# 44 small products behind TensorE's last one, ahead of its closing branch

## The chip, the cores and the metric

The kernel runs on one core of one Trainium2 chip. The metric is the device time of one execution in microseconds. The kernel before was run three times; the times given are the median of these runs and their lowest and highest.

## The reference

Attention with normalised queries and keys over 8 batches, 12 heads, 448 tokens and 64 numbers a head, and behind it a two-layer network on the 768 columns of all heads together. Cut to what matters:

```python
def rmsnorm(x, g):
    return x / np.sqrt(np.mean(x * x, axis=-1, keepdims=True) + 1e-06) * g
scores = (1 / np.sqrt(64)) * rmsnorm(q, g_q) @ rmsnorm(k, g_k).transpose(0, 1, 3, 2)
attn = softmax(scores)                       # over the keys
x = (attn @ v)                               # [8, 12, 448, 64] -> [8, 448, 768]
xn = (x - mean(x)) / np.sqrt(var(x) + 1e-06) * g_ln
out = x + np.maximum(xn @ w_ch1, 0) @ w_ch2  # 768 -> 3072 -> 768
```

## The kernel before

The order of all engines' instructions is written out by hand. A first part (`run_first`) does the attention of the first batch from a written list; it also holds small products of the identity with itself (line 532, tile `psW`). A second part (`run_rest`) goes through the eight batches: for each, it emits the chunks of the network (`mlp_chunks`) and, between them, the steps of the next batch's attention (`upto`). TensorE computes scores (L405), attention times values (L458, L460), the first layer (L798, tile `psH`) and the second (L821, tile `psP`). ScalarE does the exponentials (L421) and the ReLU (L801), VectorE the additions (L757, L804), and stores go out from SP's queue, ScalarE's and GpSimd's (L956, L959).

The last batch has no attention beside it. In `run_rest` its chunks are emitted one after the other (the branch `if b + 1 == B`), and then the loop ends. Its last group of tokens (`mlp_group` with `final`) closes with one product cut in two halves of 192 columns: 12 products each (L821), each half followed by one addition on VectorE (L757) and by a store in two parts, one from SP and one from ScalarE (L959).

In two of these chunks, `flag` computes whether all intermediate values stayed within the limits for which this fast way holds. It writes one whole number (`sh.flag`); its last step is a product into a tile `psF` with the tag `oB` of the PSUM pool `ps_o` (L1035) and a comparison on VectorE (L1036).

Behind `run_rest`, each of the five engines loads the flag into a register (L1218, `nc.values_load`) and takes a branch (L1219, `tc.If`). With the flag at 0, as here, the branch skips the general path `_general`, whose code stands in the program between the fast way and the closing code. Behind the branch, each engine has an instruction that waits until its own earlier instructions are done. SP then waits, one after the other, for all DMAs and all engines' counts, and all five meet at a barrier (both under L1246). The program ends behind a second such barrier. A hint for the branch (`mark_branch_hint_location`) is called among the last chunks; in the built program, and in the trace, the five hints stand at the start of the streams (L1246, at 0.9 to 1.0 us).

In the profile's rows, PE is TensorE's product unit, PEld its weight loads and PEldq or PEq its instruction stream; DVEq, ACTq, POOLq and SPq are the streams of the other engines.

Of the kernel before, what the change touches and what calls it, by code (L numbers as in the profile page):

```python
# [8 lines left out]
FP32 = mybir.dt.float32  # L9
# [17 lines left out]
EXP_BIAS = -4.0  # L27
DVE_KG, POOL_HI, POOL_DUP, ACT_Q = (0, 6), (1, 2, 3, 4, 5, 6, *range(8, 25)), (3, 4, 5, 6), (0, 2, 4, 5)
POOL_SQUARE, POOL_LO = ((2, 1), (4, 0), (6, 0)), (5, 6)

# [59 lines left out]
class _Fast:  # L92
# [870 lines left out]
    def upto(self, target):  # L963
        while self.pos < min(target, len(self.steps)):
            for call in self.steps[self.pos]:
                call()
            self.pos += 1
# [8 lines left out]
    def run_rest(self):  # L976
        steps, mark, upto = self.steps, self.mark, self.upto
        for b in range(B):
            tail = TAIL[b]
            chunks = list(self.mlp_chunks(b))  # L980
            total = sum(c for c, _ in chunks)
            if b + 1 == B:
                for i, (_, emit) in enumerate(chunks):
                    if i == len(chunks) - 55:
                        self.tc.mark_branch_hint_location("general", "LikelyTaken", [ENG.PE, ENG.DVE, ENG.SP, ENG.Activation, ENG.Pool])
                    for call in emit if isinstance(emit, list) else [emit]:
                        call()
                    if i in FLAG_AT:
                        self.flag(FLAG_AT.index(i))
                break  # L990
            start, goal = self.pos, mark[b + 1]
            done, items = 0.0, None
            if b == 0:
                ops, last = self.weight_sums()
            elif b == 1:
                ops += last
            left = sum(c > 0 for c, _ in chunks)
            for cost, emit in chunks:
                if not cost:
                    emit()  # L1000
                    continue
                for i, call in enumerate(emit):
                    call()
                    if i + 1 < len(emit):
                        upto(int(min(goal, start + (goal - start) * (done + cost / 2) / (total - 960 * tail))))
                left -= 1
                if (left < 10 if b == 0 else b == 1) and ops:
                    ops.pop(0)()
                done += cost
                upto(int(min(goal, start + (goal - start) * done / (total - 960 * tail))))  # L1010
                if self.pos >= goal:
                    if items is None:
                        items = self.ln_list(b + 1)
                        if b == 0:
                            items.insert(items.index("X1") + 1, "y8")
                            self.ln["y8"] = self.prep_ops(8)["y"]
                        for u, (x, _, _) in enumerate(UNITS):
                            if x == b + 2 and self.late_v(u):
                                self.ln[f"Z{u}"] = self.prep_ops(u)["z"]
                                items.append(f"Z{u}")  # L1020
                    if items and (items[0][0] != "X" or left <= DOWN):
                        x = items.pop(0)
                        self.ln[x]()
            for x in items:
                self.ln[x]()
            if b + 2 == B:
                upto(len(steps))
# [223 lines left out]
```

## Time and profile before

| | us |
|---|---|
| median of 3 runs | 581.99 |
| lowest and highest | 581.73, 582.49 |
| profiled execution, its own time | 579.58 |
| span of the profiled execution, first to last instruction | 578.0 |
| TensorE busy | 559.5 (97%) |
| VectorE busy | 381.7 (66%) |
| ScalarE busy | 364.4 (63%) |
| GpSimd busy | 207.0 (36%) |

Busy times count computing instructions; loads of registers, branches, waits and the issue of DMAs are not in them. All times in rows are microseconds from the first instruction, unless a row says otherwise. The profiled execution's own time is 1.6 us longer than its span, and the runs without a profile are 2.4 us longer than that.

The rows of the fetch of instructions (queues `q8` and `q14`, kind "instruction") give packets, megabytes and the share of 16 DMA engines' time. Where such a row is shown for a stretch of time, the share is of that stretch.

### The profile page before, as it was taken

Reading aid. Unit: us, or ns where it says so; the run is one execution under the profiler, and the core shown is the slowest. Engines: PE = TensorE matmul, PEld = TensorE weight load, DVE = VectorE, ACT = ScalarE, POOL = GpSimd, SP = SyncE. Lnnn points to the kernel's source line nnn. Section 1 sums busy time; section 2 is a strip of 40 time slices with the busy share of each in tenths; the row PEclk is TensorE's granted clock in tenths of the full one; section 3 lists DMA queues with packets and bytes.
Section 4 is the critical chain, followed back from the end, with each engine's and each line's share of the span. In section 5 each row is a group of like instructions: output and inputs, shape, how many; then the busy total and the mean of one; then the engine's idle time right before and its main releaser. Section 6 shows DMA issues by size and latency. Waiting matters only on the chain.

```text
span 578.0 us, 13670 instructions
## 1 busy us (share of the span) xinstructions
PE 559.5 (97%) x5446; PEld 411.9 (71%) x5446; DVE 381.7 (66%) x826; ACT 364.4 (63%) x674; POOL 207.0 (36%) x224
## 2 busy tenths in 40 slices
PE   5788999999999999999999999999999999999997
PEld 4556666687686867777677768777777777878684
DVE  6989567699657586845667586854756743664424
ACT  5998787447675779557775588637777477323130
POOL 5885636404440620654241521644242320020000
PEclk9999999999999999999999999999999999999999
DMA  8999999958672876969663798958743390030201
GB/s 206 251 238 222 214 207 165 193 147 137 124 131 77 158 127 145 127 148 121 121 106 48 184 134 136 128 143 122 145 64 65 119 113 1 1 110 1 83 2 58
DMA packets 178329, 72.59 MB, mean 126 GB/s; under 512 B 138212, under 2 KB 173220, under 8 KB 178260
## 3 DMA queue, kind: packets, MB, share of 16 engines
q1 hardware_dynamic: 133876, 52.52, 44.1%
q0 software_dynamic: 43440, 18.52, 25.2%
q8 instruction: 44, 0.72, 0.5%
q10 hardware_dynamic: 944, 0.62, 0.4%
q14 instruction: 25, 0.20, 0.1%
HBM read 52.76 MB, written 11.01 MB: 110 GB/s over the span
## 4 chain that ended last, share of the span: by engine, by line
PE 77%; DVE 1%; issue 0%; DVEq 0%
PE psH L798 33%; PE psP L821 30%; PE psS L405 7%; PE oA L458 4%; PE oB L460 1%; PE psS L411 1%; DVE qn L83 0%; DVE w2s L763 0%; DVE ssq L265 0%; DVE w L763 0%; DVE xn L662 0%; DVE hS L804 0%; DVE x L475 0%; DVE xl L757 0%; DVE xl L480 0%
## 5 line engine op out<-in xcount | busy, mean ns | idle before, releaser
L421 ACT ACTIVATE E<-psS,rr_all 128x448 f16<-128x448 f32 x336 | 204.6, 634 | 47.3 <-PE psS L405 40.3
L798 PE MATMUL psH<-xnT,w 128*128 128x256 f16 (+1 forms) x2016 | 225.7, 261 | 0.0
L798 PEld LDWEIGHTS <-w 128*128 128x128 f16 x2016 | 172.8, 98 | 24.3 <-issue 4.9
L801 ACT ACTIVATE hS<-psH 128x512 f16<-128x512 f32 x150 | 89.8, 599 | 97.2 <-PE psH L798 93.0
L821 PEld LDWEIGHTS <-hS 128*128 128x128 f16 x1080 | 100.0, 98 | 57.3 <-issue 1.1
L821 PE MATMUL psP<-w,hS 128*128 128x384 f16 x672 | 127.0, 326 | 0.0
L405 PE MATMUL psS<-qU,kU 128*128 128x448 f16 x288 | 100.9, 352 | 5.0 <-ACT E L421 3.2
L458 PEld LDWEIGHTS <-E 128*128 128x128 f16 x1008 | 70.3, 98 | 35.8 <-issue 2.8
L279 POOL TENSOR_TENSOR k<-k,gprod 128x896 f32<-128x896 f32 x18 | 38.9, 2160 | 139.5 <-ACT khl L259 113.2
L804 DVE TENSOR_TENSOR hS<-hS 128x512 f16<-128x512 f16 (+1 forms) x119 | 60.2, 512 | 19.3 <-ACT hS L801 17.8
L821 PE MATMUL psP<-w2s,hS 128*128 128x384 f16 (+1 forms) x408 | 69.9, 321 | 0.0
L458 PE MATMUL oA<-v,E 128*128 128x65 f16 x864 | 66.9, 193 | 1.1 <-ACT E L421 0.6
L757 DVE SCALAR_TENSOR_TENSOR x<-psP,rs_all,x 128x384 f32<-128x384 f32 x60 | 36.4, 617 | 42.4 <-PE psP L821 41.8
L460 PE MATMUL oB<-v,E 128*128 128x65 f16 x288 | 52.0, 193 | 0.1
L832 POOL TENSOR_TENSOR x<-x,hS 128x384 f32<-128x384 f32 x21 | 23.4, 1126 | 76.1 <-ACT hS L900 75.5
L473 DVE RECIPROCAL rec_all<-oA 128x6 f32<-128x6 f32 x48 | 9.2, 193 | 53.6 <-PE oA L458 53.5
L216 POOL DMA_DIRECT2D v<-in_v_dram x54 | 41.5, 781 | 4.0 <-PE oB L460 2.7
L405 PEld LDWEIGHTS <-kU 128*128 128x128 f16 x288 | 28.0, 98 | 11.1 <-issue 2.2
L900 ACT ACTIVATE hS<-hS,rs_all 128x384 f32<-128x384 f32 x27 | 14.6, 604 | 33.0 <-DVE hS L804 33.0
L460 PEld LDWEIGHTS <-E 128*128 128x128 f16 x336 | 32.4, 96 | 0.4 <-DVE xl L480 0.3
L83 DVE SCALAR_TENSOR_TENSOR qn<-q,rr_all 128x256 f16<-128x256 f32 (+2 forms) x69 | 24.8, 420 | 7.2 <-ACT rr_all L269 7.1
L265 DVE TENSOR_REDUCE ssq<-khl 128x14 f32<-128x896 f32 (+1 forms) x24 | 25.5, 1061 | 5.0 <-ACT khl L259 4.8
(145 smaller groups left out, 616.6 us busy)
## 6 DMA issues: line engine op xcount, KB each, us to landing
k<-in_k_dram SPq DMA_DIRECT2D x19, 384.0 KB, 4.2
q<-in_q_dram SPq DMA_DIRECT2D x18, 384.0 KB, 3.9
out_dram<-x SPq DMA_DIRECT2D x14, 384.0 KB, 3.0
w<-in_moe_w_ch_dram POOLq DMA_DIRECT2D x3, 1536.0 KB, 14.3
v<-in_v_dram POOLq DMA_DIRECT2D x54, 64.0 KB, 4.4
out_dram<-x POOLq DMA_DIRECT2D x9, 384.0 KB, 2.7
w<-in_moe_w_ch_dram POOLq DMA_DIRECT2D x1, 2304.0 KB, 22.5
w<-in_moe_w_ch_dram POOLq DMA_DIRECT2D x2, 1152.0 KB, 14.4
```

What stands on the lines that cost most here:

```text
L216: nc.gpsimd.dma_start(out[:, :, j, 0:D], main[:, :, j])
L265: nc.vector.tensor_reduce(out=c["ssq"][:, n], in_=c["sq", n], axis=AX.X, op=ALU.add)
L279: (nc.vector if u in DVE_KG else nc.gpsimd).tensor_tensor(out=c["t"][1], in0=c["t"][1], in1=sh.gprod.unsqueeze(1).broadcast_to([128, g, D] ...
L405: nc.tensor.matmul(ps[0][:, 0:S], c["main"][:, ts(i, 128)], c["q"][:, ts(h, S)], start=True, stop=True)
L421: nc.scalar.activation(out=o, in_=x[:, 0:S], func=AFT.Exp, scale=self.units[u][3][:, g:g + 1], bias=EXP_BIAS)
L458: nc.tensor.matmul(oA[:, t, cs], E[:, ts(t, 128)], rhs, start=(i == 0 and t == 0), stop=(i == 6 and t == 2))
L460: nc.tensor.matmul(oB[:, cs], E[:, 320:448], rhs, start=(i == 0), stop=(i == 6))
L757: self.nc.vector.scalar_tensor_tensor(out=x, in0=ps, scalar=self.rs[:, b, t:t + 1], in1=x, op0=ALU.mult, op1=ALU.add)
L798: nc.tensor.matmul(ps[:, i], sh.w1[:, dc, ts(f + i, 128)], self.xnT[:, dc, 256 - N:256], start=(i == 0 and dc == 0), stop=(i == k - 1 and ...
L801: nc.scalar.activation(out=hT[:, f:f + k], in_=ps, func=AFT.Relu)
L804: nc.vector.tensor_tensor(out=out, in0=a, in1=c, op=op)
L821: nc.tensor.matmul(bank[x][:, c], a[:, f], w[:, f, c], start=(start and f == 0), stop=(stop and f == HALF - 1))
```

## The change

Behind the last chunk of the last batch, TensorE gets 44 products of the 128x128 identity with itself, each with its weight load: 88 instructions. They write a new tile `psW` of the pool `ps_o` with the tag `oB`, which nobody reads. In the built program they stand behind TensorE's last product and ahead of its load of the flag; TensorE's count of products that it and SP wait for at the end is 44 higher. The streams of the other engines up to their branches are the same.

```diff
+END_WORK = 44
 ...
                     if i in FLAG_AT:
                         self.flag(FLAG_AT.index(i))
+                psW = self.ps_o.tile([128, 128], FP32, tag="oB", name="psW")
+                for _ in range(END_WORK):
+                    self.nc.tensor.matmul(psW, self.sh.id16, self.sh.id16, start=True, stop=True)
                 break
```

In the changed kernel the added products are line 993, and the lines behind the loop stand four further down.

## The prediction

> **What bounds the kernel now.** I read the chain that ended last first, then the end of the timeline, then the closing instructions by line, then the DMA queues in narrow stretches. The page and the chain, in order of time:
>
> ```profile
> span 578.0 us, 13670 instructions
> ...
> PE 77%; DVE 1%; issue 0%; DVEq 0%
> ...
> 564.38 9.79 PE psP L821 x72
> ```
>
> TensorE's products carry the chain to 574.17 us (564.38 + 9.79). What follows is 3.9 us in which no product runs, and the change lies in there. The timeline of the last microseconds (start, length, engine, line, operation):
>
> ```profile
> 572.02 2.14 PE L821 MATMUL psP<-w2s,hS 128*128 128x192 f16 x24
> ...
> 573.65 1.47 SPq L959 DMA_DIRECT2D out_dram<-xl  x2
> 574.20 0.42 DVE L757 SCALAR_TENSOR_TENSOR xl<-psP,rs_all,xl 128x192 f32<-128x192 f32 x1 [0.57 <-PE psP L821]
> ```
>
> The last product ends at 574.16; VectorE's last addition takes 574.20 to 574.62; the last store is issued behind it. Then every engine takes the branch that skips the general path (L1219) and meets at the barrier (L1246). These two lines, as the views of one source line show them (duration in ns min/median/max, first and last start in us):
>
> ```profile
> L1218 PEldq TENSOR_LOAD <-flag x1: 487/487/487, 572.5 to 572.5; - x1
> ...
> L1219 POOLq COMPARE_BRANCH  x1: 67/67/67, 537.1 to 537.1; - x1
> ...
> L1219 PEldq COMPARE_BRANCH  x1: 2287/2287/2287, 573.1 to 573.1; - x1
> L1219 DVEq COMPARE_BRANCH  x1: 84/84/84, 575.1 to 575.1; - x1
> L1219 SPq COMPARE_BRANCH  x1: 78/78/78, 575.2 to 575.2; - x1
> L1219 PEldq EVENT_SEMAPHORE  x1: 51/51/51, 575.5 to 575.5; - x1
> L1219 DVEq EVENT_SEMAPHORE  x1: 21/21/21, 575.7 to 575.7; - x1
> L1219 ACTq COMPARE_BRANCH  x1: 73/73/73, 576.2 to 576.2; - x1
> L1219 ACTq EVENT_SEMAPHORE  x1: 17/17/17, 576.7 to 576.7; - x1
> ```
>
> ```profile
> L1246 PEldq DRAIN  x1: 248/248/248, 575.6 to 575.6; - x1
> ...
> L1246 SPq DRAIN  x2: 7/10/13, 577.1 to 577.2; - x2
> ...
> L1246 POOLq EVENT_SEMAPHORE  x1: 17/17/17, 577.2 to 577.2; - x1
> ```
>
> TensorE's branch takes 2.29 us, where the other engines' take 0.07 to 0.08. Yet TensorE stands at the barrier at 575.9 (575.6 + 0.25). The barrier is passed at 577.2, when SP comes, 1.3 us after TensorE. SP's own waits in the stretch from 574.6 to the end, and the landing of the last two pairs of stores:
>
> ```profile
> SPq L1246 <- DMA out_dram<-xl: 0.3, 1, 0.3
> ...
> DMA to landing us min/median/max: 2.1/2.5/2.9
> ```
>
> So the end is set by VectorE's last addition, the issue of the last store at 574.6 and its landing 2.1 to 2.5 us later. A TensorE that comes to the barrier before 577.2 costs nothing, and one that comes earlier than now gains nothing.
>
> **The change, part by part.** It adds 44 weight loads and 44 products at the end of TensorE's stream, ahead of its load of the flag and its branch. The other engines' streams up to their branches are as they were. The two waits that count TensorE's products (TensorE's instruction behind the branch, and one in SP's list at the barrier) now count 44 more, so both stand behind the last of the added ones. Their output tile was last used by the flag's small product, long done, so nothing holds the first of them. Nothing of the numerical work stands behind them: VectorE's last addition waits for a product ahead of them.
>
> *How long they run.* The kernel has the same product, line 532, at its beginning, in two speeds:
>
> ```profile
> 5.98 2.74 PE L532 MATMUL psW<-id 128*128 128x128 f16 x24
> ...
> 15.05 1.06 PE L532 MATMUL psW<-id 128*128 128x128 f16 x16
> ...
> L532 PE MATMUL psW<-id x16: 219/219/219, 15.1 to 15.9; 128*128 128x128 f16 x16
> ```
>
> From the second group the pace is (1.06 - 0.22) / 15 = 0.056 us; from the first, which follows the start of the kernel, about (2.74 - 0.3) / 23 = 0.106. The last microseconds look like the second, with TensorE busy throughout and at full granted clock (columns: TensorE busy, ..., PEclk, DMA share, GB/s):
>
> ```profile
> 560.00:570.00 10.00, 10.00 (x75) 7.20 (x74) 5.64 (x11) 1.79 (x3) 0.00 (x0) 1.00 0.00 1
> ```
>
> I take 0.056: 44 x 0.056 = 2.46 us, and TensorE's last product ends at 574.16 + 2.46 = 576.62. The slower pace would make it 44 x 0.106 = 4.7 us and 578.8; it is kept as a rival.
>
> *When the branch comes.* TensorE's load of the flag started at 572.5, while this many weight loads of the last product were still to start (the line's instructions from 572.53 on):
>
> ```profile
> L821 PEld LDWEIGHTS <-hS x17: 97/98/98, 572.5 to 573.8; 128*128 128x128 f16 x17
> ```
>
> So the instruction stream runs some 17 products ahead of the array. In the changed kernel the load starts with 17 added products to go: the last starts at 576.62 - 0.22 = 576.40, 17 x 0.056 = 0.95 earlier is 575.45. The branch starts 0.6 later as now (572.5 to 573.1), at 576.05, instead of 573.1.
>
> *How long the branch takes then.* This is the disputed term. A branch that finds what it needs takes 0.08, and the next instruction starts 0.5 to 0.6 after the branch did (DVE 575.1 to 575.7, ACT 576.2 to 576.7). TensorE's took 2.29. The reason I read from the instruction queue. Queue q8 is TensorE's, by its rate: products and weight loads between its packets, and the stretches in which packets stand (first the stretch 573.0 to 573.1, then 576 to 577):
>
> ```profile
> q8 instruction: 44, 0.72, 0.5%
> ...
> 539.20:554.75 15.55, 15.55 (x126) 12.03 (x124) 4.96 (x10) 4.18 (x7) 0.00 (x0) 1.00 0.13 51
> 554.75:573.05 18.30, 18.30 (x140) 13.35 (x139) 8.93 (x17) 3.35 (x6) 0.00 (x0) 1.00 0.01 3
> ...
> q8 instruction: 1, 0.02, 58.3%
> ...
> q14 instruction: 2, 0.02, 6.6%
> q8 instruction: 1, 0.02, 6.4%
> ```
>
> 44 packets of 16 KB; between the packets at 539.20, 554.75 and 573.05 stand 250 and 279 instructions. The packet at 573.05 is thus the next one due by the stream's pace, not one that the branch at 573.1 called for. No further q8 packet comes before 576, while TensorE is through its branch at 575.4; so the packet of 573.05 carries the code behind the branch, and the branch stood until it was usable. That packet is called by the stream's position ahead of the added products and keeps its time. A branch at 576.05 comes 0.6 us after 575.4, the moment at which its code was there, and takes the short form.
>
> *The sum.* Next instruction at 576.05 + 0.5 to 0.6 = 576.6; it also waits for the last product, 576.62; from it to the barrier takes 0.4 (575.5 to 575.9), so TensorE arrives at 577.0 to 577.1. SP's list needs TensorE's count at about 577.0, and has it at 576.7. The barrier's own time, 577.2, stands: the cover is 0.1 to 0.2 us, where it was 1.3. Change: 0, and every 0.1 us that TensorE is later than reckoned beyond that is 0.1 us on the whole. In the profiled execution (span 578.0, its own time 579.58) that is 579.6; the runs shown have a median of 581.99, 2.4 above it, an offset that I carry over. With 0.1 for the thin cover the forecast is 582.1 us, 0.02% over 581.99. A measurement of this kernel can tell about 0.2%, 1.16 us, from no change.
>
> *A rule that speaks against this.* The branch row is 2.29 us, at a target far behind in the code. The Trainium skill, page "Runtime: NRT & Kernel Launch", section "Instruction fetch mechanics", says that a taken branch whose target is outside the two pages held must fetch it by DMA before execution goes on; by that the stall follows the branch wherever it is put, and the sum would be about 583.5, which is the first rival below. The order of the packets speaks against it here.
>
> **The rivals.**
>
> *Slower: the branch costs 2.29 us wherever it stands.* TensorE goes on at 576.05 + 2.29 + 0.06 = 578.4 and is at the barrier at 578.8; the barrier slips by 1.55 us: 583.5 (+0.27%). It decides as soon as the branch takes over about 0.7 us. For it: the one TensorE branch in the trace took that long. Against: the packet stands before the branch. Chance 0.16.
>
> *The branch waits for the array to run dry.* Now it ends 1.25 us behind the last product (574.16 to 575.41). Then it ends at 576.62 + 1.25 = 577.87, TensorE arrives at 578.3, +1.1: 583.1 (+0.19%). Against: VectorE's branch, 0.5 us behind its last addition, shows nothing alike. Chance 0.08.
>
> *The slow pace.* TensorE's last product at 578.8, arrival at 579.2, +2.0: 584.0. Chance 0.04, since TensorE has no pause ahead of these products.
>
> *A shift of the closing code.* 88 more instructions move what follows them against the 16 KB packets, so that the closing code may need one packet more. Price between 0 and one stall of 2.29 us; nothing in the trace places the boundary. I take 1 us: 583.0. Chance 0.06.
>
> *Faster: the fetch behind the branch leaves the last stores' way.* Each branch is followed by one packet about 1.1 to 1.4 us later. TensorE's, in 576 to 577, holds one of 16 DMA engines for 6.4% of 16 us = 1.0 us, just as the last stores land; put off by 0.6 us it falls behind them. If a store stood wholly behind it, the gain is 1.0 us: 581.0 (-0.17%). Against: SP waited 0.3 us for a landing in all, which leaves little to win. Chance 0.10.
>
> That the added products are dropped or stand elsewhere is ruled out by the order of the built program.
>
> **How the numbers follow.** The forecast, no change, has the rest: 0.56. Faster by over 0.2% is half of the faster rival and a little of the spread of the runs: 0.09. Slower by over 0.2% is most of the first rival (0.14), the slow pace (0.04), half the shift (0.03), some of the second (0.03) and a little spread (0.02): 0.26. Within: 0.65. The range takes in the forecast with the spread of the runs (581.73 to 582.49), the second rival and the first, and leaves out the slow pace and the far end of the faster one: 581.2 to 583.6.
>
> **What would show it.** In the changed profile: 44 products of line 993 at 0.056 us each; TensorE's flag load near 575.45 and branch near 576.05; the q8 packet still in 573.0 to 573.1, the next one later than now by about the 0.6 us of the branch; TensorE's drain near 576.8 and SP still last. A short branch proves the reading of the packet; a branch of 2.29 us, or one that ends 1.25 us behind the last added product, proves a rival and puts TensorE last at the barrier. Wrong altogether would be a change of over 1.2 us with TensorE at the barrier before SP.

## The result, and the profile after

The changed kernel took 580.77 us (median of 11 runs, 579.83 to 582.38), the kernel before 581.93 us (11 runs, 581.73 to 583.02). The ratio is 0.9978, 95% interval 0.9968 to 0.9988: it is faster by 1.2 us, where no change was forecast, and 580.77 lies 0.4 us under the range. The ratios leave out one run, 653.68 us of `sp_dve_late` below, at a granted clock of 0.852 instead of 0.99 to 1.

The profiled execution of the changed kernel hardly differs from that of before: 579.83 against 579.58. The first rows are of its page (span, and the chain by engine), the next of the added line, and then of the load of the flag, the branch and the barrier (lines 1222, 1223 and 1250 there):

```profile
span 578.3 us, 13758 instructions
...
PE 87%; DMA 5%; SPq 3%; DVE 3%; issue 1%; POOL 1%; ACT 1%; ACTq 0%; POOLq 0%
```

```profile
L993 PE MATMUL psW<-id x44: 219/219/219, 574.2 to 576.6; 128*128 128x128 f16 x44
```

```profile
L1222 PEldq TENSOR_LOAD <-flag x1: 588/588/588, 575.7 to 575.7; - x1
```

```profile
L1223 PEldq COMPARE_BRANCH  x1: 393/393/393, 576.4 to 576.4; - x1
...
L1223 PEldq EVENT_SEMAPHORE  x1: 51/51/51, 576.9 to 576.9; - x1
```

```profile
L1250 SPq DRAIN  x2: 7/10/13, 577.4 to 577.5; - x2
...
L1250 PEldq DRAIN  x1: 8/8/8, 577.0 to 577.0; - x1
L1250 POOLq EVENT_SEMAPHORE  x1: 17/17/17, 577.5 to 577.5; - x1
```

The last product of the work ended 0.24 us later in this execution than in the one of before (574.40 against 574.16), and with that taken off everything is close to where the prediction put it: the branch 0.39 us long instead of 2.29, TensorE at the barrier at 577.06, SP last at 577.47. So these two profiles explain no gain at all. The gain shows in the other executions of the kernel before. All of its first eleven runs took 581.73 or more; the profiled one, 579.58, had fallen out of that row by over 2 us. A second trace of it, `before_again` below, took 581.48. Here are SP's waits at its end, its branch and barrier, and the landing of the stores that were issued from 574.7 on:

```profile
SPq L1246 <- DMA out_dram<-xl: 2.0, 3, 1.4
SPq L1246 <- PEq L1246: 0.7, 2, 0.5
SPq L1246 <- DMA out_dram<-x: 0.3, 1, 0.3
```

```profile
L1219 PEldq COMPARE_BRANCH  x1: 1792/1792/1792, 573.5 to 573.5; - x1
L1219 PEldq EVENT_SEMAPHORE  x1: 51/51/51, 575.4 to 575.4; - x1
```

```profile
L1246 SPq DRAIN  x2: 7/10/13, 579.0 to 579.1; - x2
L1246 PEldq DRAIN  x1: 8/8/8, 575.5 to 575.5; - x1
```

```profile
DMA to landing us min/median/max: 3.1/3.4/3.6
```

SP waits 2.3 us for landings (2.0 + 0.3), against 0.3 us in the prediction's profile, and it comes to the barrier 4.6 us after the last product instead of 3.1. TensorE has been there since 575.5, 3.6 us before SP. (The 0.7 us put down to TensorE are two waits in the barriers, 0.14 and 0.51 us, after SP has come; they stand in the first profile with the same length.) So it isn't TensorE's arrival that costs, but the stores. What holds them stands in the DMA queues of the same trace, first in the stretch 576.6 to 577.6, then 577.6 to 578.4 (packets, megabytes, share of 16 engines' time in the stretch):

```profile
q10 hardware_dynamic: 44, 0.02, 9.1%
q14 instruction: 2, 0.02, 6.2%
q8 instruction: 1, 0.02, 5.8%
q1 hardware_dynamic: 6, 0.00, 1.4%
...
q14 instruction: 1, 0.01, 4.0%
q10 hardware_dynamic: 5, 0.00, 3.0%
q1 hardware_dynamic: 4, 0.00, 2.5%
```

TensorE's packet of 16 KB starts at 576.65 and takes 0.93 us (5.8% of 16 us). The last store on each of the two queues q1 and q10 has 64 packets of data. They are through by 576.7 and 577.0 but for four each, one sixteenth: these follow only when the packet has ended at 577.58, and land 1.3 to 1.4 us after the other fifteen parts. In the changed kernel's trace the packet has moved out of the way, behind the last landing at 577.2, and no part of the stores is late; its rows for 576.5 to 577.4 and for 577.5 to 578.3, and SP's waits:

```profile
q10 hardware_dynamic: 44, 0.02, 11.3%
q14 instruction: 2, 0.02, 7.5%
q1 hardware_dynamic: 1, 0.00, 0.0%
...
q8 instruction: 1, 0.02, 7.4%
```

```profile
SPq L1250 <- DMA out_dram<-xl: 0.4, 1, 0.4
```

Up to the last product the traces of the two kernels hardly differ: it ends at 574.16, 574.54 and 575.04 us in the three of before and at 574.40 and 574.54 in the two of the changed kernel. From there SP comes to the barrier after 4.57 and 4.24 us in the two later traces of before, and after 3.07 and 3.22 in the changed kernel's. That is 1.0 to 1.5 us, beside the 1.2 us between the medians.

### The profile page after: what moved, and what is told of

It reads as the page before. It is cut to its first block, busy times and chain, and to the rows that moved or that the text cites. A ratio compares the mean times of both kernels' runs of the same rounds, so it can differ in the third digit from the quotient of the medians.

```text
span 578.3 us, 13758 instructions
## 1 busy us (share of the span) xinstructions
PE 562.5 (97%) x5490; PEld 414.9 (72%) x5490; DVE 381.7 (66%) x826; ACT 364.5 (63%) x674; POOL 207.1 (36%) x224
## 4 chain that ended last, share of the span: by engine, by line
PE 87%; DMA 5%; SPq 3%; DVE 3%; issue 1%; POOL 1%; ACT 1%; ACTq 0%; POOLq 0%
PE psH L799 34%; PE psP L822 30%; PE psS L406 8%; PE oA L459 5%; PE psC L729 4%; DMA k<-in_k_dram 2%; PE oB L461 2%; PE psS L412 2%; SPq L155 2%; DMA q<-in_q_dram 1%; PE psH L719 1%; SPq L147 1%; DMA w<-in_v_dram 1%; DVE ssq L266 1%; DMA w2s<-in_k_dram 1%
```

## The experiments

The theories: A, that TensorE's branch meets its code too late and TensorE is last at the barrier; B, that the packet which follows TensorE's branch must not fall among the last stores; C, that the difference lies ahead of the last product; D, in the later runs, that the products themselves matter. One table for all traces, worked out from their records; times are in us, counted from the end of the last product of the work (line 821, 822 in the changed kernel). "Packet" is the q8 packet that follows the branch, "landing" the last part of the last stores, "TensorE" and "SP" their arrivals at the barrier. Each row's times come from one execution; the ratio compares all runs of that kernel with runs of the kernel before made beside them, and is not the quotient of two medians.

| run | profiled us | packet | landing | TensorE | SP | ratio of the runs, 95% |
|---|---|---|---|---|---|---|
| before | 579.58 | 2.61 | 2.78 | 1.72 | 3.06 | |
| before_again | 581.48 | 2.11 | 4.29 | 0.98 | 4.57 | 0.9999, 0.9989 to 1.0009 |
| before_third | 581.63 | 1.71 | 3.96 | 0.83 | 4.24 | 0.9997, 0.9986 to 1.0009 |
| after | 579.83 | 3.53 | 2.79 | 2.67 | 3.07 | 0.9978, 0.9968 to 0.9988 |
| after_again | 580.11 | 3.13 | 2.94 | 2.68 | 3.22 | 0.9980, 0.9969 to 0.9991 |
| shift24 | 583.47 | 0.43 | 4.34 | 0.21 | 4.62 | 1.0004, 0.9988 to 1.0020 |
| end22 | 582.22 | 2.32 | 4.69 | 1.55 | 4.91 | 0.9990, 0.9978 to 1.0003 |
| end30 | 582.25 | 2.80 | 5.23 | 2.10 | 5.45 | 0.9980, 0.9968 to 0.9992 |
| end88 | 582.69 | 5.47 | 3.11 | 5.12 | 5.22 | 1.0014, 1.0006 to 1.0023 |
| pe_loads4 | 581.71 | 3.87 | 4.32 | 3.44 | 4.54 | 0.9985, 0.9973 to 0.9997 |
| pe_loads5 | 580.33 | 4.08 | 2.90 | 3.58 | 3.67 | 0.9989, 0.9969 to 1.0008 |
| dve_late | 581.88 | 3.12 | 2.89 | 2.68 | 3.17 | 0.9985, 0.9975 to 0.9994 |
| sp_dve_late | 581.10 | 3.30 | 3.44 | 2.81 | 3.67 | 0.9994, 0.9983 to 1.0004 |
| nohint_pe | 582.99 | 5.47 | 5.61 | 4.93 | 5.89 | 1.0002, 0.9990 to 1.0013 |

**The two kernels again.** `before_again`, no edit.

> The kernel before, unchanged, for a second trace of it and for the spread of its runs. The eleven runs of it stood at 581.73 to 583.02 us, its profiled execution at 579.58, over 2 us below all of them, so that execution may not show what the others do. Theory A (late branch): in a usual run TensorE's closing branch is stalled longer than the 2.29 us of the profile and TensorE comes last to the barrier, up to 1 to 2 us after SP; a trace with a longer total would show TensorE's branch over 3.5 us. Theory B (stores): a usual run has the instruction packet behind TensorE's branch in the way of the last stores; a longer trace would show SP waiting longer for their landing. Theory C (elsewhere): the difference between the runs lies ahead of the last product, and the tail is the same. Time: 581.9 against itself, ratio 1.000.

Median 581.93. The trace is shown above: B's sign, a wait for landings, with TensorE's branch shorter than in the first profile and TensorE early. A has fallen for this kernel: up to its arrival at the barrier, SP waits for no product or branch of TensorE. `before_third`, no edit, run last:

> The kernel before once more, for a third trace. Of the two so far one has the packet behind TensorE's branch at 2.61 and the last landing at 2.78 us behind the last product, in 579.58; the other at 2.11 and 4.29, in 581.48. Theory B: if this trace is of 581.3 or more, packet at 2.0 to 2.4 and a last landing over 4; if below 580.5, packet at 2.6 or later. Time 581.8, ratio 1.000.

Median 581.83; packet at 1.71, landing at 3.96. The expectation was a packet at 2.0 to 2.4 and a landing over 4; both came a little earlier, in the same order. SP's waits in it:

```profile
SPq L1246 <- DMA out_dram<-xl: 1.9, 2, 1.5
```

`after_again`, the changed kernel without an edit:

> The changed kernel again, for a second trace. Ratio to before 0.9978 (0.9968 to 0.9988) as measured, 580.8 us. Theory A: TensorE's branch short (0.4 us) in every trace, TensorE at the barrier before SP or within 0.1 us of it. Theory B: the packet behind the branch after the last landing. Theory C: differences between its traces lie ahead of the last product, by up to 2 us.

Median 580.74, ratio 0.9980. Packet after the landing again.

**The branch left early, its code ready.** `shift24` puts 48 instructions in front, in a pause, and none at the end.

```diff
-H5 a2 e1 g1 S0.2 c2 S0.3 k1 l1 z0 d2 e2 m1 K1 S0.4 i2 H16 S0.5 S0.6 Q1 g2 H5 J8 b3 l2 j2 k2 c3
+H5 a2 e1 g1 S0.2 c2 S0.3 k1 l1 z0 d2 e2 m1 K1 S0.4 i2 H16 S0.5 S0.6 H24 Q1 g2 H5 J8 b3 l2 j2 k2 c3
```

> The kernel before with 24 products of the identity (48 instructions) put into a pause of TensorE near 17 us, and nothing at the end: the packet that holds the code behind the branch is called 48 instructions earlier, some 3 us before the branch instead of just ahead of it, while the branch keeps its early place at 573. Theory A (the branch met its code too late): branch short, TensorE early at the barrier, the whole gain or more: 580.0 to 580.8 us, ratio 0.9965 to 0.998. Theory B (the packet behind the branch must come after the stores): branch short at 573.1, so that packet comes at about 574.4 to 575.5, full in the stores' way: no gain, 581.9 to 582.9. Theory C (the gain is not in the tail): 581.9 plus the cost of the 24 products, at most 0.3.

```profile
L1219 PEldq COMPARE_BRANCH  x1: 398/398/398, 575.5 to 575.5; - x1
```

```profile
SPq L1246 <- DMA out_dram<-x: 1.7, 1, 1.7
SPq L1246 <- PEq L1246: 0.7, 2, 0.5
SPq L1246 <- DMA out_dram<-xl: 0.6, 2, 0.3
```

The stall is gone (0.40 us) and TensorE is at the barrier 4.4 us before SP, and there is no gain: 582.59, ratio 1.0004. The packet now comes at 0.43 and takes 1.4 us, to 1.84, among the stores before the last. One sixteenth of the store of `x` goes on at 1.82 and lands at 3.64, the other fifteen have landed by 1.53, and the last landing is as late as before, 4.34. (ScalarE's last store is 1.73 us in its issue here, 0.50 in the traces of before; why is open.) The last product ends at 576.5 in this trace, 1.4 to 2.3 us later than in those of before, so the time alone could hide a gain in the tail. What refutes A is the tail itself: a short branch and an early TensorE win nothing there.

**How many products.** `end22`, `end30` and `end88` change one number.

```diff
-END_WORK = 44
+END_WORK = 22   # 30, 88
```

> The changed kernel with 22 added products instead of 44: the branch is reached at about 574.8 instead of 576.05. By the profile of before its code is there at 575.4, so the branch would be stalled by 0.6 us and TensorE be at the barrier at 575.9 as before. Theory A with a code that comes at 575.4: gain as with 44, 580.8; with a code that comes later in usual runs: the same. Theory B (the delay of the packet behind the branch matters): that packet stays at 576.8, no gain, 581.9. Theory C: 581.9 or 580.8, no order with the number.

> The changed kernel with 30 added products: the branch at about 1.1, the packet behind it at about 2.75 us behind the last product. In the traces so far a packet at 2.11 and 2.32 held the last landings to 4.3 and 4.7, one at 2.61 did not (2.78). Theory B with its edge between 2.4 and 2.6: the whole gain, 580.8, and TensorE early at the barrier. An edge later than 2.75: no gain, 581.8; in between, runs of both kinds.

> The changed kernel with 88 added products instead of 44: the last ends 4.9 us behind the last product of the work, TensorE comes to the barrier at about 5.3 us, 2.2 after SP. Every theory: that much slower than the changed kernel, 582.9, ratio to before 1.0015; it prices a TensorE that is too late. If it stays at 580.8, TensorE's arrival isn't on the path.

With 22 the packet comes at 2.32, still in the way, and the trace has the last landing at 4.69; 581.95, no gain that can be told from none. With 30: 580.50, the whole gain (0.9980). Its trace, though, is of its longest run (582.25): there SP's store of `x` (L957), the third from its last, was 1.17 us in its issue instead of 0.34 to 0.69 in the traces of before, so that SP's last store was issued 0.5 us later and landed at 5.23. What held it at first was not TensorE's packet: the late parts begin at 3.27 and 3.30, when two packets of 8 KB of other engines end (2.49 to 3.27 and 2.75 to 3.30). TensorE's (2.80 to 4.05) runs beside the rest of them, and the trace doesn't part its share. The trace with 22 has the same long issue (1.05), and both kinds of packet in the way: late parts begin at 2.98, when one of 8 KB ends, and at 3.29, close to the end of TensorE's at 3.32. So these two traces don't place the edge for TensorE's packet; it depends on when the stores go out in a run. With 88 TensorE is the last at the barrier, and SP waits for it:

```profile
SPq L1250 <- PEq L1222: 2.2, 1, 2.2
```

582.57, 1.8 us more than with 44 where 2.1 was expected. So the added work can be too long, too.

**The delay without products.** `pe_loads5` and `pe_loads4` put further loads of the flag on TensorE in place of the 44 products.

```diff
+                for _ in range(5):   # 4
+                    self.nc.values_load_multi_w_load_instructions(self.sh.flag[0:1, 0:1],
+                        engines=[ENG.PE], min_val=0, max_val=1, bass_reorder=False)
                 break
```

> The kernel before with five more loads of the flag on TensorE ahead of its own load and branch, in place of the 44 products: no product is added, the branch alone comes later, by some 5 x 0.59 = 2.95 us, at about 1.9 us behind the last product (2.0 in the changed kernel, -1.0 before). Theory B (the 16 KB packet behind TensorE's branch must come after the last stores have landed): that packet at 3.0 us or later behind the last product, the last landings by 2.9, ratio 0.997 to 0.999 as with the 44 products, 580.8 us. Theory D (the products themselves matter, by keeping the array busy): ratio 1.000, 581.9.

> The kernel before with four more loads of the flag on TensorE instead of five, still without the 44 products. With five, TensorE came to the barrier at 3.58 us behind the last product, half a microsecond after SP's list was through, and the trace shows the last landings at 2.90 with the packet at 4.08. With four the branch comes at about 2.2, TensorE at about 2.9, and the packet at about 3.3. Theory B: as the changed kernel, 580.8, ratio 0.998. Theory D (the products matter): 581.8, ratio 1.000.

Each load took longer than reckoned, with a check of its value behind it: the branch came at 2.94 (five) and 2.64 (four). With five the landing is early (2.90) and TensorE itself is late (3.58); 581.30, the interval holds no change. With four 580.92, ratio 0.9985 (0.9973 to 0.9997): a gain without a single product, against D, though its interval ends close to 1. The four's trace is of one of its longest runs (581.71); there the last four packets of the stores stand behind a packet of 8 KB of another engine's branch (2.33 to 3.16), not behind TensorE's.

**The other engines' packets.** `dve_late` adds one such load on VectorE to the changed kernel, `sp_dve_late` one on SP as well.

```diff
+                self.nc.values_load_multi_w_load_instructions(..., engines=[ENG.DVE], ...)
+                self.nc.values_load_multi_w_load_instructions(..., engines=[ENG.SP], ...)   # sp_dve_late
                 break
```

> The changed kernel with one more load of the flag on VectorE ahead of its own: VectorE's branch, and the 8 KB packet behind it, come about 0.9 us later (packet at 3.1 instead of 2.25 us behind the last product, past the landings at 2.8 to 2.9). Theory B for all packets: 0.2 to 0.5 us faster than the changed kernel, 580.3 to 580.6. If an 8 KB packet of 0.5 us does no harm, or stands on a DMA engine on which no part of a store is last: 580.8 as the changed kernel.

> The same, and one more load on SP between its last store and its branch, 0.9 us. Both 8 KB packets past the landings. Against it stands that SP's own list of twelve waits, 0.75 us long, starts at 2.5 instead of 1.6 and ends at 3.3 instead of 3.0. Theory B for all packets: gain of both less 0.3: 580.0 to 580.6. If the packets do no harm: 581.1.

580.79 and 581.33. VectorE's packet moved to 2.91 and nothing was won over the changed kernel (in that trace the last product itself ended 1.9 us later than in the changed kernel's, at 576.28, so the spread of the runs has a part ahead of the tail, as C has it); with SP's load SP comes later (3.67). For the packets of 8 KB, B isn't borne out by times; that they can be in the way is seen in the traces of `end22`, `end30` and `pe_loads4`, all with a long issue of SP's store of `x` (1.05 to 1.17 us). The trace of `sp_dve_late` has such an issue too (1.12), but no instruction packet between the last product's end and 2.90: its stores were through by 2.77 and landed by 3.44, against 4.32 to 5.23 in those three.

**Without TensorE's hint.** `nohint_pe`:

```diff
-mark_branch_hint_location("general", "LikelyTaken", [ENG.PE, ENG.DVE, ENG.SP, ENG.Activation, ENG.Pool])
+mark_branch_hint_location("general", "LikelyTaken", [ENG.DVE, ENG.SP, ENG.Activation, ENG.Pool])
```

> The kernel before without the branch hint for TensorE alone. If the packet at -1.1 to -1.7 us is the hinted target, then without the hint it holds the code that follows in line, the branch has to call its target itself (packet at about 0.2) and is stalled to about 2.5, TensorE at the barrier at about 3.0, the packet behind the branch at about 3.7, past the landings: the early packet may hold earlier stores, the last ones land by 3: 580.7 to 581.5. If the hint at the start of the stream does nothing: packets and time as before, 581.8.

```profile
L1219 PEldq COMPARE_BRANCH  x1: 5587/5587/5587, 573.9 to 573.9; - x1
```

```profile
SPq L1246 <- DMA out_dram<-x: 0.9, 1, 0.9
SPq L1246 <- DMA out_dram<-xl: 0.8, 2, 0.5
```

The branch takes 5.59 us, more than the 3.4 expected. No packet of 16 KB comes in the 18 us ahead of it; two come behind its start, at 0.11 and 0.95, overlap and take 2.2 and 2.0 us. So with the hint at the head of the stream the code is called in time, and the packet before the branch carries its target, as the prediction read it; that the hint puts it there, the prediction did not see. The rule of the Trainium skill ("Runtime: NRT & Kernel Launch", section "Instruction fetch mechanics") that a branch to a page not held waits for its fetch agrees with this run; with the hint in place the changed kernel's branch took 0.39. The time, 581.88, is that of before and not the 580.7 to 581.5 expected: TensorE comes at 4.93, SP at 5.89 in the trace, with the stores held by the two packets. With two packets, two of the sixteen parts of a store are late: of the store of `x`, fourteen land by 1.36 and the others at 4.40 and 4.67.

No kernel here beats the changed one by more than its interval; 30 products do as well as 44.

## Why the prediction was wrong

- *The added products* (0.056 us each, the last ends at 2.46): as reckoned. *The branch's place* (2.0 against 1.9 reckoned): right. *Its length*: 0.39 instead of 0.08, but the sum used the next instruction, 0.5 after the branch's start, and that is as reckoned. *The packet called by the stream's position* came 1.69 us before the last product's end, ahead of the branch as reckoned, but 0.6 us earlier than in the prediction's profile; in the two later traces of before it stood at 1.63 and 1.78, so that profile had it late. In all three traces of before the branch ends 2.4 us after the start of this packet, which bears out that it waited for it. *TensorE in time* (577.06 against 577.47): right, with a cover of 0.4 instead of 0.1 to 0.2 us.
- *The step that failed is the one behind the sum:* "the runs shown have a median of 581.99, 2.4 above it, an offset that I carry over". It was not an offset. Where spans of single runs are listed, they stand 1.6 us under their times, as the profiled one's does, so that 581.99 meant a span of 580.4 and not 578.0. The 2.4 us lay inside the span, and the sum had no term for them. The profiled execution was one in which the branch had been stalled for 2.29 us; its packet came at 2.61 and just missed the stores. In the two later traces the stall was 1.79 and 1.63 us, the packet came at 2.11 and 1.71, and the stores paid 1.2 to 1.5 us. In the sum's own terms: SP's wait for landings was put at 0.3 us and the effect of a later packet on it at nothing ("Change: 0"); in `before_again` that wait is 2.3 us, 0.4 in the changed kernel's trace. I took a tail with nothing to win for the usual one. Such a tail is rare rather than impossible: of 102 later runs of the kernel before, 5 took less than 580.5 us.
- *The rival that came true* was the last, "the fetch behind the branch leaves the last stores' way": mechanism right, price 1.0 against 1.2 measured, chance 0.10. That the price came so close is partly luck: it was read from an execution in which the packet held nothing back (the stores' data were through at 2.28, the packet began at 2.61), and it reckoned with a whole store behind the packet, where in the later traces it was one sixteenth of two. What spoke against it, "SP waited 0.3 us for a landing", was true of that execution alone; in `before_again` it is 2.3.
- *"One that comes earlier than now gains nothing"* holds for TensorE's arrival (`shift24`), and *"TensorE later costs"* too (`end88`). But the branch has a second effect, the packet behind it, that reaches the stores through the DMA engines.
- *The slower rivals:* a branch of 2.29 us wherever it stands, and one that ends 1.25 us behind the last product, have fallen (0.39 us; it ended 0.06 us before the last added product did). The slow pace and the shifted code did not show.

What is shown: the order of packet and landings in the traces, the gain by a delay with products and (by a smaller margin) without, no gain by a ready branch or by too short a delay. That the packet and the late parts use the same DMA engine is not shown directly, since the records as kept don't name it; it is inferred from the four packets of 64, from their starting when the packet ends, and from the two late sixteenths behind two packets. Open is what sets the 0.34 to 1.17 us of SP's issue, how much the packets of 8 KB cost, and the spread of 2 us within each kernel.

## What to carry to other kernels

An engine that is done early isn't free of effect: its closing branch calls code by DMA, and that packet can fall among the last stores, whose landing ends the kernel. Time such a branch so that its packet comes behind the last stores while the engine still reaches the barrier first. And set the profiled execution's time beside the spans and times of all runs before arguing from its tail: when it lies outside of them, it may not show what they do.

## What was not expected of the hardware

In these traces the end of a closing branch was followed by one instruction packet, of 16 KB for TensorE (0.7 to 1.4 us later, 0.93 to 1.45 us long) and of 8 KB for the others (0.3 to 0.8 us long). One packet of 0.93 us held back the last sixteenth of two stores by 1.2 to 1.4 us (`before_again`, `before_third`). TensorE's branch took 0.39 to 0.50 us with its code ready, 1.6 to 2.3 when the code was on its way, and 5.59 when it had to call it itself.
